# A reordered attention-and-experts kernel: new places in its fixed order, routing by pairs of batches, a product in 64-row tiles, late weights asked for earlier

## The chip, the cores and the metric

The kernel runs on one core of one Trainium2 chip. The metric is the device time of one execution in microseconds (us), the median of the runs shown. TensorE is called PE, VectorE DVE, ScalarE ACT, GpSimd POOL and SyncE SP, as in the profile.

## The reference

A Nyström attention over 8 batches of 8 heads, 576 positions and 64 features is followed by a layer of 8 experts. `q_lm` and `k_lm` are means over 18 neighbouring positions (32 landmarks).

```python
A = sm(q, k_lm); Bm = sm(q_lm, k_lm); C = sm(q_lm, k)      # softmax of scaled scores
Z = Bm.T / (norm1(Bm) * norminf(Bm) + 1e-6)
for _ in range(6):
    Z = 2 * Z - Z @ Bm @ Z                                  # Newton steps
x = (A @ Z @ C @ v)                                         # heads side by side: 4608 x 512
logits = x @ w_gate                                         # 8 experts
e = argmax(logits); gate_w = softmax(logits)[e]; eom = sigmoid(x @ w_output_gate)[e]
out = gate_w * eom * (relu(x @ w1[e]) @ w2[e])              # each token through its one expert
```

All tensors are float32. `w1` is 8 x 512 x 1024 and `w2` is 8 x 1024 x 512.

## The kernel before

The kernel has two stages. The first computes attention and routing. It works in 16 **units** (`u`): a batch and one half of its heads (4 heads on 4 x 32 partitions). `load_qk` and `load_v` bring the unit's q, k and v through the SP queue. `sums` adds groups of positions to landmarks on POOL (k) and DVE (q). `turn3` transposes three 128 x 128 pieces at a time on PE and `keep3` copies them from PSUM on ACT (nine transposes and three copies each for q and k). `c_scores`, `c_max`, `c_exp`, `c_turn`, `c_keep`, `values` and `keep_values` make C v; `a_scores` to `a_back` make the normalized A, transposed back, which stays in `ATs` until its batch is done.

Per **batch** (`b`), `b_scores` to `b_c` make B. `p_mm` and `p_next` are seven Newton steps, each a set of 32 x 32 matmuls on PE and an update on DVE. `z_blocks` spreads the result into block-diagonal form (`ZB`) on POOL; `z_turn`, `gates` and `logits` compute the gate logits straight from it. `x_mm` computes rows of x, 128 at a time in five pieces (the last of 64 rows), `x_out` converts them to bf16 on ACT and writes them to the DRAM table `x_rows`. `choose` finds the expert of each token, `count` adds counts on POOL, `ranks` and `places` find each token's place among its expert's tokens, `onehot` makes the matrices St, and `coef_in` to `coef` make the two factors of a token and write them to `x_rows` too.

After attention comes a closing part: from the counts, the first tile of each expert (`base`), each token's tile (`pj`), and with St a product `pinv` that inverts the placing, so that `gat_i` holds for each of 43 tiles of 128 places the row of `x_rows` to fetch. `tile_w` holds each tile's expert.

The second stage goes over 36 to 43 tiles. `load` gathers 128 rows by an indirect DMA on POOL's queue, `turn_x`, `up`, `turn` and `down` run the two matrix products in bf16, and an indirect DMA scatters the rows to `out`.

All weights stand in one SBUF tensor, `wall`, of eight slots of 2 MB. Slots 4 to 7 serve as **homes** of attention's buffers first: q and k (`nats`), partial sums (`t9s`), v (`vSs`) and the matrices of `ATs`. `load_expert(e)` asks for an expert's weights on POOL's queue, casting to bf16; each request stands behind what still reads its slot.

What sets the order: every step is a small function, recorded with a place. The list is sorted by place and each engine's instructions stand in that order; an engine's queue is strictly in order, and nothing is moved afterwards. A unit is `P = 12` places long; for example

```python
at(t - P + 1.5 + 0.4 * n, turn3, u, 0, n)
at(t + 0.0, c_scores, u)
at((NU + 4) * P if e == E - 4 else u * P + P + 3.3, lambda e=e, u=u: load_expert(e, ATs[u]))
```

The closing part is not in the list; it is recorded behind all of it. `load_expert` begins with two one-element casts from a tile that a late step writes, which hold the requests back: experts 0 to 3 at units 1, 3, 5 and 7, experts 5 to 7 after unit 15, expert 4 after the last product.

PSUM has eight banks: two for scores (`s`), two for transposes (`t`), two for small products (`m`, two buffers), one for Newton (`n`) and one for x (`px`).

Of the kernel before, what the change touches and what calls it, by code (L numbers as in the profile page):

```python
# [22 lines left out]
F32 = mybir.dt.float32  # L23
# [14 lines left out]
def kernel(  # L38
# [37 lines left out]
    def load_expert(e, after):  # L76

        for c in (0, W1):
            nc.gpsimd.tensor_copy(wall[:1, e, c:c + 1], after[:1, :1])
        nc.gpsimd.dma_start(out=wall[:, e, :W1].rearrange("p (c f) -> p c f", f=F),  # L80
                            in_=moe_w1[e].rearrange("(c p) f -> p c f", p=128))
        nc.gpsimd.dma_start(out=wall[:, e, W1:].rearrange("p (c d) -> p c d", d=HD),
                            in_=moe_w2[e].rearrange("(c p) d -> p c d", p=128))
# [20 lines left out]
    nc.gpsimd.iota(pcol, pattern=[[1, 1]], base=0, channel_multiplier=1, allow_small_or_imprecise_dtypes=True)  # L104
    tok = gp.tile([128, B, TB], F32)
# [5 lines left out]
    cum = gp.tile([128, T + 1, E], BF16)  # L111
    nc.vector.memset(cum[:, 0], 0.0)
    oh = gp.tile([128, T, E], BF16)
# [12 lines left out]
    lgs = [gp.tile([128, TB, m], F32, name=f"lg{i}") for i in range(2)]  # L126
# [17 lines left out]
    with tc.tile_pool(name="attn_c", bufs=1) as cp, \  # L144
# [4 lines left out]
        mask64 = cp.tile([128, HH, D], F32)  # L149
        nc.vector.memset(mask64, 0.0)  # L150
        for h in range(HH):
            nc.vector.memset(mask[h * m:(h + 1) * m, h, :], 1.0)
            nc.vector.memset(mask64[h * m:(h + 1) * m, h, :], 1.0)
        bones = mask.rearrange("p h l -> p (h l)")
        wgs = cp.tile([128, HH, 2 * E], F32)
        for hf in range(2):
            nc.sync.dma_start(out=wgs[hf * D:(hf + 1) * D, :, :E],
                              in_=moe_w_gate[hf * HH * D:(hf + 1) * HH * D].rearrange("(h d) e -> d h e", d=D))
            nc.sync.dma_start(out=wgs[hf * D:(hf + 1) * D, :, E:],
                              in_=moe_w_output_gate[hf * HH * D:(hf + 1) * HH * D].rearrange("(h d) e -> d h e", d=D))  # L160
# [9 lines left out]
        nats = [home(E - 1 - i // 3 * 2, i % 3, GD).rearrange("p (k d) -> p k d", d=D) for i in range(6)]  # L170
        t9s = [home(e, 6, GD // 2).rearrange("p (k d) -> p k d", d=D) for e in (E - 1, E - 3)]
        VD = HH * VJ * D
        vSs = [home(E - 2, i, VD)[:VA * m].rearrange("p (h j d) -> p h j d", h=HH, j=VJ) for i in range(2)]
# [86 lines left out]
        def values(u):  # L260
            nc.vector.reciprocal(sts[u][:, 2:3], sts[u][:, 1:2])
            sts[u, 0] = pV = ps.tile([128, 192], F32, tag="m", bufs=2, name="pV")
# [47 lines left out]
        def b_scores(b):  # L310
            pBs[b] = pB = ps.tile([128, 2, m], F32, tag="m", bufs=2, name="pB")
# [21 lines left out]
        def b_cols(b):  # L333
            pBs[b] = pS = ps.tile([128, 2, m], F32, tag="m", bufs=2, name="pS")
            nc.tensor.matmul(pS, lhsT=bones, rhs=XWs[b][:, :, :W])
# [28 lines left out]
        def z_blocks(b):  # L364
            ZBs[b] = sb.tile([128, 2, HH, D], F32, tag="ZB", name="ZB")
            for hf in range(2):
                nc.gpsimd.tensor_tensor(
                    ZBs[b][:, hf], mask64,
                    XWs[b][:, hf, :].rearrange("p (h d) -> p h d", h=1).to_broadcast([128, HH, D]), op=MUL)


        def z_turn(b):
            ZTs[b, 0] = pZ = ps.tile([128, 192], F32, tag="m", bufs=2, name="pZ")
# [6 lines left out]
        def gates(b, hf):  # L380
            ZTs[b, hf] = pG = ps.tile([128, 2 * E], F32, tag="m", bufs=2, name="pG")
            for h in range(HH):
                nc.tensor.matmul(pG[hm(h), :], lhsT=ZTs[b][hf * D:(hf + 1) * D, hm(h)],
                                 rhs=wgs[hf * D:(hf + 1) * D, h, :])

        def keep_gates(b, hf):
            nc.scalar.copy(Gs[b % 2][:, hf, :2 * E], ZTs.pop((b, hf)))

        def logits(b):
            pLs[b] = pL = ps.tile([128, TB, m], F32, tag="m", bufs=2, name="pL")  # L390
# [8 lines left out]
        def choose(b):  # L399
            lg, t0, t1, pL = lgs[b % 2], b * TB, (b + 1) * TB, pLs.pop(b)  # L400
# [3 lines left out]
            sm = sms[b] = sb.tile([128, 8, TB], F32, tag="sm", name="sm")  # L404
            w3 = w3s[b] = sb.tile([128, 2, TB, E], F32, tag="w3", name="w3")
            ohb = oh[:, t0:t1]
            nc.vector.tensor_reduce(sm[:, 0], lg[:, :, :E], axis=X, op=MAX)
            nc.vector.tensor_tensor(w3[:, 0], lg[:, :, :E], b_e(sm[:, 0], TB), op=ALU.is_ge)
            nc.vector.scalar_tensor_tensor(out=w3[:, 0], in0=w3[:, 0], scalar=-8.0, in1=b_t(e8, TB),
                                           op0=MUL, op1=ADD)  # L410
            nc.vector.tensor_reduce(sm[:, 1], w3[:, 0], axis=X, op=ALU.min)
            nc.vector.tensor_tensor(ohb, b_t(row[:, :E], TB), b_e(sm[:, 1], TB), op=ALU.is_equal)
            nc.vector.memset(ohb[64:, TB - 1], 0.0)
# [6 lines left out]
        def ranks(b):  # L420
            t0, t1 = b * TB, (b + 1) * TB
            prk = prks[b] = ps.tile([128, TB, E], F32, tag="m", bufs=2, name="prk")
            prf = prk.rearrange("p t e -> p (t e)")
            nc.tensor.matmul(prf, lhsT=U, rhs=oh[:, t0:t1].rearrange("p t e -> p (t e)"), start=True, stop=False)
            nc.tensor.matmul(prf, lhsT=ones, rhs=cum[:, t0:t1].rearrange("p t e -> p (t e)"),
                             start=False, stop=True)

        def places(b):
            t0, t1, sm, w3 = b * TB, (b + 1) * TB, sms[b], w3s.pop(b)
            nc.vector.tensor_tensor(w3[:, 1], prks.pop(b), oh[:, t0:t1], op=MUL)  # L430
            nc.vector.tensor_reduce(sm[:, 2], w3[:, 1], axis=X, op=ADD)
            smi = sb.tile([128, 2, TB], I32, tag="smi")
# [3 lines left out]
            nc.vector.tensor_copy(pjl[:, t0:t1], smi[:, 1])  # L436
            nc.vector.scalar_tensor_tensor(out=psl[:, t0:t1], in0=pjl[:, t0:t1], scalar=-128.0, in1=sm[:, 2],
                                           op0=MUL, op1=ADD)
            nc.vector.memset(psl[64:, t1 - 1:t1], -1.0)

        def onehot(b):
# [7 lines left out]
        def coef_in(b):  # L449
            lg = lgs[b % 2]  # L450
            wc = wcs[b] = sb.tile([128, 2, TB, E], F32, tag="wc", name="wc")
            nc.gpsimd.tensor_tensor(wc[:, 0], lg[:, :, :E], b_e(sms[b][:, 0], TB), op=SUB)
            nc.gpsimd.tensor_tensor(wc[:, 1], lg[:, :, E:2 * E], oh[:, b * TB:(b + 1) * TB], op=MUL)

        def coef_exp(b):
            nc.scalar.activation(out=wcs[b][:, 0], in_=wcs[b][:, 0], func=EXP)

        def coef_sum(b):
            nc.vector.tensor_reduce(sms[b][:, 3:5].rearrange("p a t -> p (a t)"),
                                    wcs.pop(b).rearrange("p a t e -> p (a t) e"), axis=X, op=ADD)  # L460

        def coef_exp2(b):
            nc.scalar.activation(out=sms[b][:, 5], in_=sms[b][:, 4], func=EXP, scale=-1.0)

        def coef(b):
            sm, t0, t1 = sms.pop(b), b * TB, (b + 1) * TB
            nc.vector.scalar_tensor_tensor(out=sm[:, 6], in0=sm[:, 5], scalar=1.0, in1=sm[:, 3], op0=ADD, op1=MUL)
            pay = sb.tile([128, TB, 2], F32, tag="pay")
            nc.vector.reciprocal(pay[:, :, 0], sm[:, 6])
            nc.gpsimd.tensor_copy(pay[:, :, 1], tok[:, b])  # L470
            nc.sync.dma_start(
                out=x_rows[t0 * 128:t1 * 128, HD // 2:].rearrange("(t p) c -> p t c", p=128), in_=pay)
# [5 lines left out]
        def x_mm(b, j):  # L478
            pX = pXs[b, j] = ps.tile([128, HD], F32, tag="px", name="pX")
            for hf in range(2):  # L480
                nc.tensor.matmul(pX[:tk(j), hf * HH * D:(hf + 1) * HH * D],  # L481
                                 lhsT=ATs[2 * b + hf][:, j * 128:j * 128 + tk(j)],
                                 rhs=ZBs[b][:, hf].rearrange("p h d -> p (h d)"))

        def x_out(b, j):
            xo = sb.tile([128, HD], BF16, tag="xo", bufs=3)
            nc.scalar.copy(xo[:tk(j)], pXs.pop((b, j))[:tk(j)])  # L487
            r0 = (b * TB + j) * 128
            nc.sync.dma_start(out=x_rows[r0:r0 + tk(j), :HD // 2], in_=xo[:tk(j)].bitcast(F32))


        plan = []

        def at(place, fn, *args):
            plan.append((place, len(plan), fn, args))

        P = 12.0
        for u in range(NU):
            t = u * P
            at(t - 4 * P + 11.9 if u > 2 else -30 + u, load_qk, u)  # L500
            at(t - 2 * P + 11.9 if u > 1 else -30 + u + 0.5, load_v, u)
            for n in range(3):
                at(t - P + 1.5 + 0.4 * n, turn3, u, 0, n)
                at(t - P + 2.6 + 0.5 * n, keep3, u, 0, n)
# [244 lines left out]
```

## Time and profile before

| | |
|---|---|
| median of 3 runs | 456.54 us (454.12 to 457.53) |
| profiled execution: its time | 459.6 us |
| profiled execution: its span | 457.8 us |
| granted PE clock, mean | 0.917 |
| busy PE, DVE, ACT, POOL | 359.2, 250.3, 160.0, 221.8 us |
| read from and written to HBM | 67.58 MB, 15.25 MB |

Busy time is the time in which at least one instruction of the engine ran, so overlapping matmuls are counted once. The slices cut the span in 40 parts of 11.4 us with the busy tenths of each. In a group's line, the count after x is of instructions (a float32 matmul appears as two), then the busy us and the mean ns of one, and behind the bar the engine's idle time just before them with what ended it. "Issue" means that nothing the profile shows was waited for.

### The profile page before, as it was taken

How to read it: one execution, taken by the hardware profiler on the slowest of the kernel's cores; microseconds unless marked ns; L12 is line 12 of the kernel's file. 1: busy time of each engine (PE TensorE's matmuls, PEld its weight loads, DVE VectorE, ACT ScalarE, POOL GpSimd, SP SyncE). 2: the span in 40 equal slices, each digit the busy share in tenths (PEclk: the TensorE clock that was granted, in tenths of full speed). 3: DMA queues.
4: the chain of work that ended last, by engine and by line, in shares of the span. 5: the costliest groups of instructions: out<-in, count | busy, mean ns of one | idle time of the engine just before them, and what ended most of it. 6: DMA issues, size and time to landing. Idle time of an engine off the chain costs nothing.

```text
span 457.8 us, 11307 instructions
## 1 busy us (share of the span) xinstructions
PE 359.2 (78%) x4264; PEld 212.0 (46%) x4283; DVE 250.3 (55%) x657; ACT 160.0 (35%) x373; POOL 221.8 (48%) x327
## 2 busy tenths in 40 slices
PE   0767687887888888888784534899999999999790
PEld 0444455555555555555452322455555555555450
DVE  1267766986869788686653331344544344444340
ACT  1445454455545645564321200222222222222110
POOL 2555758285672736563542255145454455444321
PEclk9878989999989999999888555999999999999996
DMA  6965999969799665321199994022222322233211
GB/s 145 251 227 168 226 262 207 263 166 233 217 243 255 175 180 139 114 48 59 27 189 222 212 215 138 24 83 93 103 95 80 105 94 92 93 95 104 74 52 37
DMA packets 41353, 66.44 MB, mean 145 GB/s; under 512 B 9953, under 2 KB 29410, under 8 KB 41282
## 3 DMA queue, kind: packets, MB, share of 16 engines
q0 software_dynamic: 17648, 31.90, 31.5%
q1 hardware_dynamic: 23634, 33.64, 26.1%
q8 instruction: 39, 0.64, 0.6%
q14 instruction: 32, 0.26, 0.2%
HBM read 67.58 MB, written 15.25 MB: 181 GB/s over the span
## 4 chain that ended last, share of the span: by engine, by line
PE 42%; DVE 21%; issue 11%; DMA 10%; POOL 7%; ACT 5%; SPq 1%; POOLq 0%; ACTq 0%; DVEq 0%
PE ph L656 13%; PE py L675 12%; DMA out_dram<-ysb 6%; PE pX L481 3%; PE pht L666 3%; DMA wall<-in_q_dram 3%; PE p L234 2%; DVE ax L287 2%; DVE At L284 2%; POOL At L290 2%; PE pV L266 2%; ACT ECT L258 2%; PE pt L642 2%; DVE st L243 2%; PE pN L349 2%
## 5 line engine op out<-in xcount | busy, mean ns | idle before, releaser
L660 ACT ACTIVATE h<-ph 128x512 bf16<-128x512 f32 x76 | 41.3, 594 | 139.4 <-PE ph L656 139.4
L682 POOL DMA_INDIRECT out_dram<-ysb x38 | 38.5, 1013 | 85.5 <-DVE ysb L681 85.5
L656 PE MATMUL ph<-wall,xT 128*128 x303 | 74.9, 391 | 4.9 <-issue 2.6
L210 PE MATMUL pT<-I,wall 128*128 128x128 f32 x288 | 50.1, 307 | 32.1 <-ACT tr L214 15.4
L675 PE MATMUL py<-wall,hT 128*128 x286 | 67.9, 379 | 0.9
L214 ACT COPY tr<-pT 128x384 f32<-128x384 f32 x96 | 43.3, 480 | 44.4 <-PE pT L210 44.3
L210 PEld LDWEIGHTS pT<-I,wall 128*128 128x128 f32 x288 | 33.9, 153 | 46.4 <-ACT tr L214 25.9
L481 PE MATMUL pX<-ZB,wall 128*128 128x256 f32 (+1 forms) x160 | 48.4, 430 | 6.3 <-ACT xo L487 6.3
L656 PEld LDWEIGHTS <-xT 128*128 128x128 bf16 x304 | 30.3, 100 | 42.7 <-issue 8.7
L634 POOL DMA_INDIRECT xs<-x_rows,gat_i x43 | 41.8, 972 | 16.0 <-issue 11.0
L668 DVE COPY hT<-pht 128x1024 bf16<-128x1024 bf16 x38 | 26.3, 691 | 39.1 <-PE pht L666 38.5
L290 POOL TENSOR_TENSOR At<-At,ax 128x576 f32<-128x576 f32 x16 | 18.6, 1161 | 55.8 <-DVE ax L287 55.8
L675 PEld LDWEIGHTS <-hT 128*128 128x128 bf16 x304 | 28.2, 98 | 27.1
L680 DVE CAST ysb<-xs 128x1 int32<-128x1 f32 x38 | 5.7, 153 | 55.6 <-DMA out_dram<-ysb 23.2
L481 PEld LDWEIGHTS pX<-ZB,wall 128*128 128x128 f32 (+1 forms) x160 | 28.0, 196 | 15.1 <-ACT xo L487 8.6
L487 ACT CAST xo<-pX 128x512 bf16<-128x512 f32 (+1 forms) x40 | 23.3, 583 | 27.9 <-PE pX L481 21.2
L681 DVE TENSOR_SCALAR ysb<-py,xs 128x512 f32<-128x512 f32 x38 | 28.3, 745 | 8.1 <-PE py L675 7.5
L197 POOL TENSOR_TENSOR wall<-wall 128x576 f32<-128x576 f32 x16 | 22.4, 1402 | 12.2 <-DMA wall<-in_k_dram 12.2
L300 POOL TENSOR_TENSOR At<-At,ax 128x576 f32<-128x576 f32 x16 | 18.5, 1156 | 19.7 <-DVE ZV L361 8.0
L349 PE MATMUL pN<-nxt 32*32 32x96 f32 x768 | 26.9, 257 | 0.5 <-DVE nxt L358 0.5
L234 PE MATMUL p<-tr,lmT 64*32 64x288 f32 x512 | 25.7, 462 | 0.8 <-ACT lmT L224 0.5
L349 PEld LDWEIGHTS pN<-nxt 32*32 32x32 f32 x768 | 16.1, 108 | 20.7 <-issue 9.0
(143 smaller groups left out, 546.1 us busy)
## 6 DMA issues: line engine op xcount, KB each, us to landing
wall<-in_moe_w_dram POOLq DMA_DIRECT2D x16, 1024.0 KB, 19.2
wall<-in_k_dram SPq DMA_DIRECT2D x16, 576.0 KB, 6.7
wall<-in_q_dram SPq DMA_DIRECT2D x16, 576.0 KB, 8.2
wall<-in_v_dram SPq DMA_DIRECT2D x48, 192.0 KB, 4.7
x_rows<-xo SPq DMA_DIRECT2D x32, 128.0 KB, 5.9
xs<-x_rows,gat_i POOLq DMA_INDIRECT x43, 4.1
out_dram<-ysb POOLq DMA_INDIRECT x38, 2.8
x_rows<-St SPq DMA_DIRECT2D x1, 516.0 KB, 4.9
```

Of the source, the lines that this page charges most:

```text
L210: nc.tensor.transpose(pT[:, k2], identity=I128, in_=nat[:, 6 * n + 2 * k2:6 * n + 2 * k2 + 2].rearrange("p k d -> p (k d)"))
L214: nc.scalar.copy(tr[u, i][:, 3 * n:3 * n + 3], tr.pop((u, i, n)))
L234: nc.tensor.matmul(p[hm(h), i, :NC], lhsT=lms[i * D:(i + 1) * D, hm(h)], rhs=rhs)
L290: nc.gpsimd.tensor_tensor(Ats[u], Ats[u], b_l(axs[u][:, 0]), op=SUB)
L349: nc.tensor.matmul(pN[hm(h), hf, :], lhsT=cur[hm(h), hf, :W], rhs=cur[hm(h), hf, :])
L481: nc.tensor.matmul(pX[:tk(j), hf * HH * D:(hf + 1) * HH * D], lhsT=ATs[2 * b + hf][:, j * 128:j * 128 + tk(j)], rhs=ZBs[b][:, hf].rearrang ...
L634: nc.gpsimd.indirect_dma_start(out=xs, out_offset=None, in_=x_rows, in_offset=bass.IndirectOffsetOnAxis(ap=gat_i[:, j:j + 1], axis=0))
L656: nc.tensor.matmul(ph[hf], lhsT=xT[:, dc, :], rhs=wf[:, bass.ds(we[j] + (dc * F + hf * 512), 512)], start=(dc == 0), stop=(dc == DCH - 1))
L660: nc.scalar.activation(out=hs[j][:, hf * 512:(hf + 1) * 512], in_=ph[hf], func=RELU)
L675: nc.tensor.matmul(py, lhsT=hT[:, fc, :], rhs=wf[:, bass.ds(we[j] + (W1 + fc * HD), HD)], start=(fc == 0), stop=(fc == FCH - 1))
L681: nc.vector.tensor_scalar(out=ysb[:, :HD], in0=py, scalar1=xs[:, HD // 2:HD // 2 + 1], scalar2=None, op0=MUL)
L682: ins = nc.gpsimd.indirect_dma_start(out=out, out_offset=bass.IndirectOffsetOnAxis(ap=token, axis=0), in_=ysb[:, :HD], in_offset=None, bou ...
```

## The change

- **Places.** All steps take their places from one table `PLACE`, with entries of their own for the last (`!`) and the one before the last (`?`) unit, batch or group. The closing part is cut into steps (`counts`, `full_tiles`, `starts`, `tiles`, `slot_cols`, `slot_tiles`, `slots`, `slot_rows`, `tile_experts`) that are in the list as well.
- **Routing.** `choose`, `ranks`, `places` and the coefficients run over groups of two batches; the last two batches are groups of one. Counts are no longer added on POOL: `oh` has a sixth, empty column per batch, `ranks` adds shifted copies in PSUM by twelve (six) matmuls, and `places` adds the running count on DVE.
- **x.** `ZB` holds two heads per 64 rows instead of four per 128. A piece of x is four matmuls over 64 rows and 128 columns, in pairs on the upper and lower half of the array into two PSUM banks; two pieces go together into one copy pair and one write. `px` has two banks, `m` one buffer. `gates` uses one set of matmuls in place of two.
- **Late weights.** The casts in `load_expert` are gone. Homes move: q and k to slots 6 and 4, v to 5, transposed q and k (`tr`) to three homes in 7; `ATs` get a pool of seven buffers. Experts 4, 6, 7 and 5 are asked for at places 181.7, 182.2, 186.0 and 192.5 (unit 15 begins at 180).
- **Start.** k and q of unit 0 are first in the SP queue, ahead of the gate weights.

```diff
-    def load_expert(e, after):
-        for c in (0, W1):
-            nc.gpsimd.tensor_copy(wall[:1, e, c:c + 1], after[:1, :1])
+    def load_expert(e):
...
-        nats = [home(E - 1 - i // 3 * 2, i % 3, GD).rearrange("p (k d) -> p k d", d=D) for i in range(6)]
+        nats = [home(E - 2 - i // 3 * 2, i % 3, GD).rearrange("p (k d) -> p k d", d=D) for i in range(6)]
-        vSs = [home(E - 2, i, VD)[:VA * m].rearrange("p (h j d) -> p h j d", h=HH, j=VJ) for i in range(2)]
+        vSs = [home(E - 3, i, VD)[:VA * m].rearrange("p (h j d) -> p h j d", h=HH, j=VJ) for i in range(2)]
-                tr[u, i] = sb.tile([128, K2, 128], F32, tag="tr", bufs=4, name="tr")
+                tr[u, i] = home(E - 1, (2 * u + i) % 3, GD).rearrange("p (k c) -> p k c", k=K2)
-            ATs[u] = home(E - 4, u % 7, S)
+            ATs[u] = sb.tile([128, S], F32, tag="AT", bufs=7, name="AT")
-            pBs[b] = pB = ps.tile([128, 2, m], F32, tag="m", bufs=2, name="pB")
+            pBs[b] = pB = ps.tile([128, 2, m], F32, tag="m", name="pB")
...
-            ZBs[b] = sb.tile([128, 2, HH, D], F32, tag="ZB", name="ZB")
+            ZBs[b] = sb.tile([128, 2, 2, D], F32, tag="ZB", name="ZB")
...
+        groups = [(b, b + 1) for b in range(0, B - 2, 2)] + [(B - 2,), (B - 1,)]
...
-        def count(b):
-            for t in range(b * TB, (b + 1) * TB):
-                nc.gpsimd.tensor_tensor(cum[:, t + 1], cum[:, t], oh[:, t], op=ADD)
...
+        def ranks(r):
+            nb = len(groups[r])
+            ns = nb * (TB + 1)
...
+            for l in range(ns):
+                nc.tensor.matmul(to[:, l * E:], lhsT=ones if l else U, rhs=at_[:, :(ns - l) * E],
+                                 start=(l == 0), stop=(l == ns - 1))
+        def places(r):
...
+            nc.vector.tensor_tensor(bt(w3[:, 1]), prk[:, :, :TB], bt(b_t(cum[:, r], nt)), op=ADD)
+            nc.vector.tensor_tensor(cum[:, r + 1], cum[:, r], prk[:, nb - 1, TB], op=ADD)
...
-        def x_mm(b, j):
-            pX = pXs[b, j] = ps.tile([128, HD], F32, tag="px", name="pX")
-            for hf in range(2):
-                nc.tensor.matmul(pX[:tk(j), hf * HH * D:(hf + 1) * HH * D],
-                                 lhsT=ATs[2 * b + hf][:, j * 128:j * 128 + tk(j)],
-                                 rhs=ZBs[b][:, hf].rearrange("p h d -> p (h d)"))
+        def x_mm(b, j0):
+            pX = pXs[b, j0] = ps.tile([128, 2, 2, 2, 2 * D], F32, tag="px", name="pX")
+            for j in range(j0, min(j0 + 2, TB)):
+                for hf in range(2):
+                    for i in range(2):
+                        pr = slice(i * D, (i + 1) * D)
+                        nc.tensor.matmul(pX[:tk(j), i, j - j0, hf], lhsT=ATs[2 * b + hf][pr, j * 128:j * 128 + tk(j)],
+                                         rhs=ZBs[b][pr, hf].rearrange("p h d -> p (h d)"))
...
+            xo = sb.tile([128, 2, HD], BF16, tag="xo")
...
+        PLACE = {
+            "load_qk": -36.3, "load_v": -14.6, "turn3 0 0": -11.2, "turn3 0 1": -10.3, "turn3 0 2": -10.0,
+            "keep3 0 0": -10.7, "keep3 0 1": -9.2, "keep3 0 2": -7.1, "turn3 1 0": -7.1, "turn3 1 1": -6.5,
...
+            "load_expert 0": 29.3, "load_expert 1": 52.9,
+            "load_expert 2": 78.3, "load_expert 3": 113.9, "load_expert 4": 181.7, "load_expert 5": 192.5,
+            "load_expert 6": 182.2, "load_expert 7": 186.0, "x_mm 0!": 38.9, "a_sum!": 8.3, "a_sum?": 7.4,
...
+        }
```

More of the change, by code (lines that the diff above doesn't have):

```diff
@@ L125 @@
         in_=blank.bitcast(F32).rearrange("p (b c) -> p b c", b=1).to_broadcast([64, B, XR // 2]))
[L126 removed]
+    lgs = [gp.tile([128, 2, TB, m], F32, name=f"lg{i}") for i in range(2)]
     for lg in lgs:
@@ L403, in choose, with lg_ @@
             nc.vector.transpose(out=lg[:64, TB - 1], in_=pL[:64, TB - 1])
[L404 to L409, printed above, removed]
+        def lg_(r, e0):
+            return lgs[r % 2][:, :len(groups[r])].rearrange("p b t e -> p (b t) e")[:, :, e0:e0 + E]
@@ new lines, in counts, with full_tiles @@
+        def counts():
+            pBs[B] = pn = ps.tile([E, 128], F32, tag="m", name="pn")
+            nc.tensor.matmul(pn, lhsT=cum[:, len(groups)], rhs=first)
+        def full_tiles():
+            ni = sb.tile([E, 128], I32, tag="ni", bufs=1)
+            nc.vector.tensor_scalar(out=ni, in0=pBs[B], scalar1=127.0, scalar2=None, op0=ADD)
+            nc.vector.tensor_scalar(out=ni, in0=ni, scalar1=7, scalar2=None, op0=ALU.logical_shift_right)
+            Bs[B] = sb.tile([E, 128], F32, tag="nf", bufs=1, name="nf")
+            nc.vector.tensor_copy(Bs[B], ni)
@@ new lines, in slot_tiles, with slots @@
+        def slot_tiles(a):
+            nc.gpsimd.tensor_tensor(tr[a][:, :, 1], lm[a],
+                                    row[:, a + 1:a + TQ + 1].rearrange("p (t j) -> p t j", j=1).to_broadcast([128, TQ, J]),
+                                    op=MUL)
+        def slots(a):
+            if a == 0:
+                pAs[B] = ps.tile([128, 2, J], F32, tag="px", name="pinv")
+            for t in range(TQ):
+                nc.tensor.matmul(pAs[B].rearrange("p a j -> p (a j)"), lhsT=St[:, a + t],
+                                 rhs=tr[a][:, t].rearrange("p a j -> p (a j)"),
+                                 start=(a + t == 0), stop=(a + t == T - 1))
@@ new lines @@
+        for b in range(B):
+            for fn in (b_scores, b_max, b_exp, b_norm, b_cols, b_c, z_blocks, z_turn, z_keep, gates, keep_gates, logits):
+                at("batch", b, B, fn)
+            for it in range(7):
+                at("batch", b, B, p_mm, it)
+                at("batch", b, B, p_next, it)
+            for j in range(0, TB, 2):
+                at("batch", b, B, x_mm, j)
+                at("batch", b, B, x_out, j)
+            at("batch", b, B, keep_logits)
+        for r, bs in enumerate(groups):
+            for fn in (choose, ranks, places, coef_in, coef_exp, coef_sum, coef_exp2, coef):
+                at("group", r, len(groups), fn)
+            for i in range(len(bs)):
+                at("group", r, len(groups), onehot, i)
@@ L563 @@
+        for e in range(E):
+            at("end", 0, 0, load_expert, e)
+        last = (NU - 1) * P
+        for fn in (counts, full_tiles, starts, tiles, slot_rows, tile_experts):
+            plan.append((last + PLACE[fn.__name__], len(plan), fn, ()))
+        for i in range(4):
+            for fn in (slot_cols, slot_tiles, slots):
+                plan.append((last + PLACE[f"{fn.__name__} {i}"], len(plan), fn, (i * TQ,)))
         with tc.manual_schedule():
```

331 lines of the change are left out of this document (157 added, 174 removed), and 14 rows, old and new, of the table PLACE.

## The prediction

> **What bounds the kernel now.** I read the page's slices first, then busy time by stage, then the timeline of the joint between the stages, then groups by shape and waits. The slices show three parts: attention (slices 1 to 20), a hole (slices 21 to 24), the experts (25 to 39).
>
> ```profile
> PE   0767687887888888888784534899999999999790
> PEclk9878989999989999999888555999999999999996
> DMA  6965999969799665321199994022222322233211
> ```
>
> Busy time in seven stretches follows: start, stretch from us, length, then PE, PEld, DVE, ACT, POOL, granted clock, DMA share, GB/s.
>
> ```profile
> 12.70:81.60 68.90, 52.27 (x829) 32.64 (x833) 43.62 (x102) 33.20 (x81) 44.85 (x63) 0.88 0.89 223
> 81.60:215.80 134.20, 111.56 (x2003) 71.68 (x1996) 106.41 (x291) 72.60 (x185) 73.92 (x123) 0.99 0.70 175
> 227.70:240.00 12.30, 10.38 (x158) 6.61 (x146) 5.73 (x25) 2.90 (x9) 6.43 (x18) 0.84 1.04 171
> 240.00:268.70 28.70, 15.07 (x102) 9.29 (x102) 12.44 (x43) 4.55 (x12) 8.77 (x18) 0.65 1.22 218
> 268.70:280.40 11.70, 0.59 (x4) 0.46 (x5) 0.81 (x5) 0.00 (x0) 8.24 (x9) 0.50 0.94 200
> 280.40:457.80 177.40, 160.75 (x1041) 86.28 (x1059) 69.95 (x147) 41.25 (x76) 72.07 (x73) 0.95 0.25 82
> ```
>
> 81.6 and 215.8 are the first reductions over the scores (L243) of units 5 and 15, so the second row is 10 units: 13.42 us each, 26.84 per batch. PE is busy 83% of it and DVE 79%: neither is full, the order and its waits share the bound. In units 0 to 4 (first row) the DMA engines are at 0.89. The rows from 240.0 to 280.4 are the hole: 40.4 us between the last Newton matmul and the first expert matmul. The timeline says why (start us, us, engine, line, idle before):
>
> ```profile
> 260.48 0.81 POOL L80 DMA_DIRECT2D wall<-in_moe_w_dram  x1 [13.21 <-issue]
> 262.20 1.77 POOL L596 TENSOR_TENSOR Va<-oj,row 128x430 bf16<-128x430 bf16 x2
> 268.49 0.20 DVE L608 SCALAR_TENSOR_TENSOR gat_i<-sl 128x43 int32<-128x43 f32 x1
> 269.72 1.07 POOL L634 DMA_INDIRECT xs<-x_rows,gat_i  x1 [3.10 <-issue]
> 278.63 0.59 PE L642 MATMUL pt<-Ib,xs 128*128 128x128 bf16 x4 [10.91 <-issue]
> ```
>
> POOL stands 13.2 us at the weight request of expert 4, whose home holds the matrices that the last product reads until 259.9. The routing table's multiply (L596) is behind it in POOL's queue. The first gather, issued at 269.72, lands only at 278.6, behind the 2 MB asked for at 260.5.
>
> **The change part by part.** The sum is made against the profiled execution: span 457.8, its time 459.6 us. The median of the runs shown is 456.54, 3.1 us lower.
>
> *Start.* The SP queue now issues k and q of unit 0 ahead of the small transfers.
>
> ```profile
> 0.81 0.76 SPq L157 DMA_DIRECT2D wgs<-in_moe_w_gate_dram  x1
> 4.82 2.08 SPq L184 DMA_DIRECT2D wall<-in_k_dram  x1
> ```
>
> That is up to 4.0 us earlier. Units 1 to 3 wait for bytes, so some comes back; I take -3 (bounds -4, -1). The first units keep their 68.9 us: they are DMA-bound and hold no product.
>
> *Product x in two 64-row tiles.* The groups by shape:
>
> ```profile
> L481 PE MATMUL pX<-ZB,wall 128*128 128x256 f32 x128 | 38.1, 425 | 5.3 <-ACT xo L487 5.3
> L234 PE MATMUL p<-tr,lmT 64*32 64x288 f32 x512 | 25.7, 462 | 0.8 <-ACT lmT L224 0.5 <-ACT EC L247 0.3
> ```
>
> L481 takes 38.1/32 = 1.19 us for one row tile: two matmuls of 256 columns, 430 columns per us. L234, on 64*32 tiles, streams 8 x 288 columns in 25.7/32 = 0.80 us: 2870 per us, 6.7 times as many with 8 tiles, so tiles do run side by side. The new form streams 4 x 128 columns on two tiles: 0.60 us if they overlap wholly, 0.71 at L234's 84%, 1.19 if not at all. I take 0.65, nearest L234. Five per batch save 2.7 us of PE. TensorEngine Tiling (Array Packing) of the Trainium skill, Tiling Modes, says that changing the tiling mode drains the array; that speaks against three visits per batch to a new mode. The trace shows idle of 0.25 to 0.33 us before weight loads at such joints, so by it up to 6 x 0.3 = 1.8 us per batch would go back, PE would be the fuller engine again at 21.7 us, and the time would be some 434. I don't add it, since the old form had joints with L349 and L234 of its own. POOL loses half of L367 (about 0.5 us per batch); ACT copies the same elements in as many pieces.
>
> *Routing by two batches.* DVE's choose (five operations near 0.20 us), places (seven near 0.17) and coefficients (0.24, 0.16, 0.19) run once per two batches on twice the elements; rows of 40 elements take 0.20 us and of 64 take 0.22, so a doubled one costs some 0.23. Places gains two additions of 0.2. Per batch: choose 1.0 to 0.6, places 1.1 to 0.8, coefficients 0.6 to 0.3: -1.0 us of DVE. POOL loses five counts of 0.2 per batch. PE gets twelve rank matmuls per two batches where it had four; at 0.10 (a weight load, L425) to 0.19 (L424) this adds 0.2 to 0.8 us per batch, I take 0.4. Merged gate matmuls save 0.1.
>
> *The period.* Per batch PE goes from 111.56/5 = 22.3 to 19.9 us, DVE from 21.3 to 20.3. DVE becomes the fuller engine. At the old share of the busiest engine (22.3/26.84 = 83%) the period is 20.3/0.83 = 24.4. All places move as well; one wait that they visibly address is this one:
>
> ```profile
> PE pT L210 <- ACT tr L214: 9.5, 16, 1.1
> ```
>
> In the window 94.8 to 202.5 PE waits 9.5 us for its own transposes' copies, 2.4 per batch, because all nine come in a row with two buffers; the new order parts them by other work. I credit 0.9 of it: 23.5 us. Bounds: 26.8 (places give nothing, DVE waits as before) and 21.4 (DVE 95% full). Five batches: 5 x 3.3 = -16.7. The same bytes must come: 155, 223 and 175 GB/s over the three stretches to 215.8 make 40.8 MB; 250 GB/s at a full share (175/0.70) needs 163 us, so 196 is reachable, but batches with a weight load already took 28.0 where others took 26.4 us. Four of those: I give back 3. Net -13.7 (bounds 0, -24).
>
> *Last unit and Newton iterations.* 215.8 to 240 keeps its seven steps; the products of batch 6 beside them shrink by half (four of 1.1 us to 0.6) and seven steps of 0.53 (PE) and 0.35 (DVE) are 6.2 us of 12.3: -2.5 (bounds 0, -5).
>
> *The tail.* From the last Newton matmul to the gather's rows, by durations of before: last update 0.35, turn 0.38, copy 0.33, gates 0.33, copy 0.28, logits 0.9, two transposes 0.5, choose 1.25, ranks 0.8, places 1.9, sum and tile counts 1.0, start matmul and one-hot 1.3, base, spread, reduce and add 1.4, four slot columns at L592's and L595's means 4 x 1.41 = 5.7, the last L596 1.0, ten matmuls 0.9, four closing operations 1.05: 19.4 us against 28.7. The products and copies of batch 7 lie between these on PE and ACT. Nothing on POOL's queue waits for the product now: expert 4's request is placed after the last reads of unit 14's q and k. -9.3 (bounds -5, -12).
>
> *Late weights and the first gather.* Experts 4 and 6 are asked for ahead of unit 15's subtraction on POOL (220.96 before), so 42 us ahead of the gather; with 215 GB/s of the slices after 229 us that is 9.0 MB, and 8.4 MB of weights plus 1.2 MB of product rows are wanted. They are nearly through. The gather took 268.7 to 278.6; free it costs 1.1 of issue and the page's median 4.1. I take 7 of 9.9: -2.9 (bounds 0, -4.7). The Trainium skill, DMA: Bandwidth & Descriptors, Queues, rings and completion order, says that an engine consumes the descriptors of one ring in order; the 8.9 us from issue to landing here agrees, and by it the gather cannot overtake the weights (with all 9.6 MB ahead of it, 44.7 us at 215 GB/s, it would land 2.7 us later than free).
>
> *Homes.* Transposed q and k get three homes in the wall for four buffers. The next writer of a home stands some five places after its reader, so I put it at nothing; without that cover PE would wait a score set, 0.8 us, in each of 16 units. A moves to buffers of its own, seven as before; the one-cell casts ahead of each weight request (0.3 us on POOL) go.
>
> *Experts.* Lines unchanged; 177.4 us stays.
>
> **Sum:** -3 - 13.7 - 2.5 - 9.3 - 2.9 = -31.4; 459.6 - 31.4 = 428.2, less 3.1 for the median: **425 us**.
>
> **The rivals.**
> *A, only the joints gain.* Tiles or places give the stretch of ten units nothing: the first rows' waits for DMA and for POOL (L290) stay. For: 26.4 us also in batches with no weight load and DMA at 0.5. Against: PE's own 2.4 us less. -3 - 0 - 1 - 9.3 - 1 = -14: 442.
> *B, the order pays more.* The period falls to 21.4 and the tail to 17: -3 - 24 - 4 - 12 - 4 = -47: 409. The DMA floor of 163 us stands just under it.
> *C, slower: the one-buffer PSUM tile.* Tag m falls from two buffers to one to pay for the product's second bank. Values, scores of B, columns, turn, gates, logits and ranks pass through it: 7.5 uses per batch, 60 in all. If PE, in order, waits at each for a copy queued late on ACT or DVE, everything behind it in PE's queue, transposes above all, waits too, and ACT and DVE for those. My 31 us are gone from 0.52 us per use; at 0.8 us it is 48 - 31 = 17 slower: 473. For: PE already waits up to 1.2 us for copies on ACT (pV for ECT, 4 times in that window). Against: in the new order each writer's reader stands before the next writer, mostly a whole step before.
> *D, the change does nothing.* If homes were freed as late as before, POOL would stand again and the order cancel out: 456. The order of POOL's queue, with no request behind the last product, speaks against it.
>
> **How the numbers follow.** My forecast 0.62, A 0.15, B 0.11, C 0.08, D 0.04. The forecast's own range, 413 to 438; to leave out no more than two in ten it reaches to A and B: 406 to 447. About 1% can be told from no change here. Forecast, A and B are faster by more: 0.88. D is same: 0.04. C is slower: 0.08.
>
> **What would show it.** Right: first transpose near 9 us; L243 every 11.8 us in mid attention; product busy about 26 us in place of 48; no POOL wait over 5 us at a weight request; 19 us from the last Newton matmul to the gather table; experts still 177 us. Wrong: a unit period above 13, idle of PE put down to readers of tag m, product busy near 48, or gathers that land over 9 us after issue.

## The result, and the profile after

The changed kernel takes 439.67 us (median of 4 runs, 438.62 to 442.59), beside 455.76 us for the kernel before on the same chip: a ratio of 0.966, 95% interval 0.960 to 0.972. It is faster, as forecast, by 16 us instead of 31; the time lies in the stated range of 406 to 447, but outside the forecast's own range of 413 to 438, and near the figure of rival A (442), though not by rival A's way. The profiled execution took 440.14 us with a span of 438.4, where the one before had 459.6 and 457.8; the stages below therefore differ by 19.4 us in sum, not by 16.

The slices of the changed kernel (11.0 us each), PE, granted clock and DMA share:

```profile
PE   5578698978888997977385346999999999999790
PEclk9968999989999699978655558999999999999996
DMA  6965999979979964219999331222322223323311
```

PE still has a hole, though a shorter one: the granted clock is down at 0.5 to 0.6 for five slices around it (208 to 263 us), and the DMA engines are full for four (197 to 241 us). Busy time by stretch, with the columns of the table before (start and end, length, PE, PEld, DVE, ACT, POOL, clock, DMA share, GB/s):

```profile
72.87:197.40 124.53, 106.55 (x2065) 71.96 (x2063) 100.89 (x263) 69.68 (x180) 72.94 (x96) 0.94 0.79 194
197.40:206.10 8.70, 6.79 (x146) 4.62 (x142) 6.96 (x19) 4.44 (x12) 4.71 (x8) 0.89 1.13 181
206.10:226.50 20.40, 12.54 (x183) 9.02 (x182) 7.50 (x29) 2.88 (x9) 4.07 (x7) 0.58 1.23 217
226.50:249.90 23.40, 12.13 (x119) 9.07 (x115) 13.61 (x42) 4.10 (x12) 5.12 (x9) 0.50 0.91 167
249.90:257.90 8.00, 0.62 (x5) 0.48 (x6) 1.89 (x8) 0.00 (x0) 4.62 (x5) 0.50 0.24 61
257.90:438.40 180.50, 160.99 (x1041) 86.12 (x1059) 69.31 (x148) 41.25 (x76) 75.67 (x77) 0.95 0.26 83
```

The boundaries are the same events as before: the first score reductions of units 5 and 15, the first and last Newton step of batch 7, the gather table, the first expert matmul. Set against the forecast, in us:

| stage | before | forecast | after |
|---|---|---|---|
| start to unit 15 | 215.8 | 199.1 | 197.4 |
| unit 15 to the last Newton step | 24.2 | 21.7 | 29.1 |
| last Newton step to gather table | 28.7 | 19.4 | 23.4 |
| table to first expert matmul | 11.7 | 8.8 | 8.0 |
| experts | 177.4 | 177.4 | 180.5 |

The units gave what was forecast and a little more. Against the forecast 12.0 us are missing: 7.4 in the second row, which should have shrunk and grew, 4.0 in the third and 3.1 in the last, less what the others gained. The first part of the second row in the kernel before, up to the first Newton step of batch 7 (the stretch that is missing among the seven of the prediction), was

```profile
215.80:227.70 11.90, 8.57 (x153) 5.04 (x149) 9.02 (x29) 4.25 (x11) 4.62 (x7) 0.88 0.13 35
```

and is now 8.7 us. So the whole loss of that row lies in the Newton steps, 20.4 us where they took 12.3. The timeline there (start us, us, engine, line, operation; in brackets the idle time before and who ended it):

```profile
218.01 1.07 ACT L512 CAST xo<-pX 128x512 bf16<-128x512 f32 x2 [10.53 <-DMA x_rows<-xo]
219.13 2.08 PE L504 MATMUL pX<-ZB,AT 64*128 64x128 f32 x16 [6.60 <-ACT xo L512]
236.07 1.07 ACT L512 CAST xo<-pX 128x512 bf16<-128x512 f32 x2 [7.19 <-DMA x_rows<-xo]
```

ACT stands 10.5 us for a free row buffer, which a write to `x_rows` still holds. PE stands 6.6 us behind it, at a product whose PSUM tile ACT has not emptied, and the Newton steps of batch 7 stand behind that product in PE's queue. Eighteen us later it happens again. The waits of ACT in the whole span (us in total, times, longest):

```profile
ACT xo L512 <- DMA x_rows<-xo: 21.8, 4, 10.5
```

In the kernel before the same wait came to 6.4 us. The four weight requests now stand at 194.95, 196.64, 202.81 and 207.19 us, and from then on the DMA engines are full while batches 6 and 7 write their rows.

### The profile page after: what moved, and what is told of

It reads as the page before. It is cut to its first block, busy times and chain, and to the rows that moved or that the text cites. A ratio compares the mean times of both kernels' runs of the same rounds, so it can differ in the third digit from the quotient of the medians.

```text
span 438.4 us, 11408 instructions
## 1 busy us (share of the span) xinstructions
PE 351.8 (80%) x4393; PEld 214.9 (49%) x4412; DVE 245.5 (56%) x623; ACT 156.1 (36%) x367; POOL 210.4 (48%) x262
## 4 chain that ended last, share of the span: by engine, by line
PE 42%; DVE 23%; DMA 15%; issue 6%; POOL 6%; ACT 3%; SPq 1%; another core or an unknown queue 1%; POOLq 0%; ACTq 0%
PE ph L718 13%; PE py L737 11%; DMA x_rows<-xo 7%; DMA out_dram<-ysb 6%; PE pht L728 3%; PE pX L504 3%; POOL At L291 3%; PE pN L350 2%; DVE wall L198 2%; PE p L235 2%; DMA wall<-in_q_dram 2%; DVE wall L199 2%; PE pV L267 2%; DVE st L244 2%; DVE ax L288 2%
## 5 line engine op out<-in xcount | busy, mean ns | idle before, releaser
L215 ACT COPY wall<-pT 128x384 f32<-128x384 f32 x96 | 44.3, 486 | 51.1 <-PE pT L211 50.5
L211 PE MATMUL pT<-I,wall 128*128 128x128 f32 x288 | 51.8, 313 | 13.2 <-DMA wall<-in_k_dram 9.7
L504 PE MATMUL pX<-ZB,AT 64*128 64x128 f32 (+1 forms) x320 | 31.1, 344 | 11.5 <-ACT xo L512 11.5
L291 POOL TENSOR_TENSOR At<-At,ax 128x576 f32<-128x576 f32 x16 | 19.5, 1220 | 35.6 <-DVE ax L288 35.6
L350 PE MATMUL pN<-nxt 32*32 32x96 f32 x768 | 28.4, 268 | 6.0 <-DVE nxt L359 5.8
L301 POOL TENSOR_TENSOR At<-At,ax 128x576 f32<-128x576 f32 x16 | 18.5, 1155 | 29.5 <-DVE st L262 17.8
L504 PEld LDWEIGHTS pX<-ZB,AT 64*128 64x128 f32 (+1 forms) x320 | 25.1, 228 | 15.3 <-ACT xo L512 12.6
L512 ACT CAST xo<-pX 128x512 bf16<-128x512 f32 (+1 forms) x48 | 22.2, 515 | 26.6 <-DMA x_rows<-xo 21.8
L728 PEld LDWEIGHTS <-h 128*128 128x128 bf16 x304 | 20.6, 99 | 12.6 <-ACT h L722 3.0
L235 PE MATMUL p<-wall,lmT 64*32 64x288 f32 x512 | 26.2, 470 | 0.6 <-ACT lmT L225 0.5
```

Of the source, the lines that this page charges most:

```text
L211: nc.tensor.transpose(pT[:, k2], identity=I128, in_=nat[:, 6 * n + 2 * k2:6 * n + 2 * k2 + 2].rearrange("p k d -> p (k d)"))
L215: nc.scalar.copy(tr[u, i][:, 3 * n:3 * n + 3], tr.pop((u, i, n)))
L235: nc.tensor.matmul(p[hm(h), i, :NC], lhsT=lms[i * D:(i + 1) * D, hm(h)], rhs=rhs)
L291: nc.gpsimd.tensor_tensor(Ats[u], Ats[u], b_l(axs[u][:, 0]), op=SUB)
L350: nc.tensor.matmul(pN[hm(h), hf, :], lhsT=cur[hm(h), hf, :W], rhs=cur[hm(h), hf, :])
L504: nc.tensor.matmul(pX[:tk(j), i, j - j0, hf], lhsT=ATs[2 * b + hf][pr, j * 128:j * 128 + tk(j)], rhs=ZBs[b][pr, hf].rearrange("p h d -> p ...
```

## The experiments

My theory T was then: the late weights, asked for earlier, share the DMA engines with the writes of x, these land late, and two row buffers are too few to hide it. R1 blamed the low clock; R2 said that 8.4 MB of weights are a floor whatever else is done.

**1. Five row buffers**

```diff
-            xo = sb.tile([128, 2, HD], BF16, tag="xo")
+            xo = sb.tile([128, 2, HD], BF16, tag="xo", bufs=5)
-            ATs[u] = sb.tile([128, S], F32, tag="AT", bufs=7, name="AT")
+            ATs[u] = sb.tile([128, S], F32, tag="AT", bufs=5, name="AT")
-            Vt = tr[a] = sb.tile([128, TQ, 2, J], BF16, tag="Vt", bufs=4, name="Vt")
+            Vt = tr[a] = sb.tile([128, TQ, 2, J], BF16, tag="Vt", bufs=3, name="Vt")
```

> The changed kernel with five buffers for the converted rows of x in place of two (room comes from the A buffers, 7 to 5, and from one buffer of the closing part). Theory T: the late weights share the DMA engines with the writes of x, each write takes some 10 us to land, ACT stands 21.1 us for a free buffer, and PE's products and Newton steps stand behind it. T expects these waits under 3 us in sum, the seven Newton steps of batch 7 in 13 us or less where they took 20.4, and about 429 us where the changed kernel has 439.7. Rival R1: PE's lower granted clock (0.55 to 0.86 there) stretches that part, and the waits of ACT lie beside it: the steps stay above 18 us and the time above 437. Rival R2: the 8.4 MB of late weights are a floor of their own: the first expert matmul cannot come before about 243 us of the span whatever the buffers, so at most 15 us are to be had, and less if the weights come later.

431.27 us, a ratio of 0.948 to the kernel before (0.940 to 0.956), which lies below the changed kernel's interval. No wait of ACT is put down to a write any more (4.0 us in two waits have no named cause). The stretches of this run, from the first Newton step of batch 7 to the first expert matmul, in the columns above:

```profile
206.00:218.60 12.60, 9.73 (x183) 6.71 (x182) 7.41 (x29) 2.97 (x9) 4.26 (x7) 0.81 1.25 221
218.60:237.60 19.00, 10.85 (x115) 7.89 (x115) 13.47 (x42) 4.11 (x12) 5.14 (x9) 0.59 1.23 223
237.60:248.30 10.70, 0.60 (x5) 0.46 (x6) 1.94 (x9) 0.00 (x0) 4.77 (x5) 0.50 0.90 168
```

The Newton steps take 12.6 us for 20.4, and the tail 19.0 us for 23.4; the forecast had said 19.4. The clock in the Newton stretch rises from 0.58 to 0.81 with no change aimed at it: here it went with PE's waits. R1 falls. Of the 12.2 us won here, 2.7 go back in the third row: the table is ready at 237.6, and the gather lands only at 246.1. That is R2's share, though the weights' queue is not the only wait in it. The gather reads the rows, and the chain that ended last shows the last write of rows (start us, us):

```profile
229.06 11.94 DMA x_rows<-xo
```

It lands at 241.0, after the table, and POOL issues the gather at 242.3, 4.7 us after the table. Without late weights (experiment 2) it issues 2.2 us after it.

**2. No late weights**

```diff
-        for e in range(E):
+        for e in range(E - 4):
             at("end", 0, 0, load_expert, e)
-            nc.vector.tensor_scalar(out=tile_w[:, :J], in0=ej, scalar1=float(E - 1), scalar2=float(WE),
+            nc.vector.tensor_scalar(out=tile_w[:, :J], in0=ej, scalar1=float(E - 5), scalar2=float(WE),
```

> The changed kernel without the four late weight requests; tiles of experts 4 to 7 go through the weights of expert 3, so that the same matmuls run. T: writes of x land in 3 to 4 us, ACT's waits for them go, Newton steps of batch 7 take 12 us or less, the tail about 19 us, the first expert matmul stands at about 243 us of the span where it stood at 257.9: about 425 us. R1: the clock is as low as before, nothing moves by more than 3 us: 437 to 443. R2 expects what T expects here or a little more.

422.69 us in a single run. The Newton steps take 12.7 us, the tail 18.1, and the first gather lands 5.3 us after its table; the first expert matmul stands at 245.1. The time from issue to landing of the rows' writes, by the view of that line, is in this run

```profile
DMA to landing us min/median/max: 2.3/3.6/11.0
```

and in the changed kernel

```profile
DMA to landing us min/median/max: 2.5/6.7/17.3
```

Both are over all 24 writes. Of the eight issued from 190 us on, beside the late weights, the median is 7.9 us in the changed kernel and 2.8 here, and the first of them, issued at 200.6 us, takes 17.3 us there and 3.9 here. So the writes land nearly three times as late beside the weights, and that is all that two buffers needed. In experiment 1 they land as late as in the changed kernel (median 8.7 from 190 us on); ACT no longer waits for them, only the gather does. T holds in both directions. Of the 17.0 us between this run and the changed kernel, 8.4 are the buffers' (experiment 1). Of the rest, 2.6 lie between table and first matmul, 0.9 in the tail, and 5.6 in the experts' stage (175.9 us against 181.5), where five experts share one slot's weights here; that part I can't put down to the late weights.

**3. The product in whole-array matmuls again**

```diff
-                    for i in range(2):
-                        pr = slice(i * D, (i + 1) * D)
-                        nc.tensor.matmul(pX[:tk(j), i, j - j0, hf], lhsT=ATs[2 * b + hf][pr, j * 128:j * 128 + tk(j)],
-                                         rhs=ZBs[b][pr, hf].rearrange("p h d -> p (h d)"))
+                    nc.tensor.matmul(pX[:tk(j), j - j0, hf].rearrange("p i c -> p (i c)"),
+                                     lhsT=ATs[2 * b + hf][:, j * 128:j * 128 + tk(j)],
+                                     rhs=ZBs[b][:, hf].rearrange("p h d -> p (h d)"))
```

(with `ZB` and its mask of four heads, as before the change, and A in six buffers)

> The changed kernel with the product x in whole-array matmuls again (128 rows by 256 columns, ZB of 256 columns, mask of four heads); two pieces still share the PSUM banks, the copies and the write; A has six buffers in place of seven. The prediction's step: the product costs PE 2.7 us more per batch and POOL 0.5 us; with PE the fuller engine again the period grows by 1.0 to 2.7 us per batch, the time by 8 to 20 us: 448 to 460. Rival: DVE and the order set the period, and the freed PE time was idle time; the time stays within 3 us of the changed kernel's.

451.97 us, ratio 0.993 (0.989 to 0.997): the tiles are worth 12.3 of the 16 us. The product's line in this run, and then in the changed kernel, from the groups (count, busy us, mean ns, idle before):

```profile
L502 PE MATMUL pX<-ZB,AT 128*128 128x256 f32 (+1 forms) x160 | 47.7, 446 | 13.8 <-ACT xo L511 13.8
```

```profile
L504 PE MATMUL pX<-ZB,AT 64*128 64x128 f32 (+1 forms) x320 | 31.1, 344 | 11.5 <-ACT xo L512 11.5
```

The units from 5 to 15 take 131.5 us here and 124.5 with the tiles. The rival, that freed PE time is idle time, falls: 7.0 us of units for some 10 us of PE. The rest of the 12.3 us is not PE time of the units: the Newton steps of batch 7 took 22.9 us in this run (20.4 with the tiles) and the tail 24.3 (23.4), again with waits of ACT for writes (18.2 us in all).

**4. Routing for one batch at a time**

```diff
-        groups = [(b, b + 1) for b in range(0, B - 2, 2)] + [(B - 2,), (B - 1,)]
+        groups = [(b,) for b in range(B)]
-    cum = gp.tile([128, B, E], F32)
+    cum = gp.tile([128, B + 1, E], F32)
```

> The changed kernel with routing for one batch at a time (eight groups of one, at the places that a group has). The prediction's step: DVE gets back 1.0 us per batch and is the fuller engine, so the period grows by 0.5 to 1.0 us: 443 to 447 us. Rival: these DVE operations fall into its idle time; within 2 us of the changed kernel's.

440.80 us, ratio 0.971 (0.962 to 0.980): not to be told from the changed kernel. The trace tells more than the time. DVE is busy 108.6 us between units 5 and 15 where it was 100.9, and unit 15 comes at 202.3 us where it came at 197.4, which would make pairing worth 4.9 us up to there. How far one trace can be trusted in this is shown by experiments 1, 7 and 8, whose kernels are the same up to the late weights: their unit 11 stands at 147.5, 150.0 and 150.7 us. So the work on DVE is sure, and the 4.9 us are not known to better than some 3. The difference doesn't show in the time, since the Newton steps of batch 7 took 12.4 us in this run, against 20.4: ACT's waits for writes came to 17.6 us here, where they were 21.8, and lay elsewhere. The expectation's step points the right way in the units, and its total was missed.

**5. The new places alone**

```diff
-            at(t + 0.0, c_scores, u)
...
+            for fn in (turn_lm, keep_lm, c_scores, c_max, c_exp, a_scores, a_max, a_sub, a_exp, a_sum, a_mul, a_back,
+                       values, keep_values):
+                by(u, NU, t, fn)
```

(`by` looks a step up in the new table; the rest of the kernel before stays)

> The kernel before with the new places for the steps of units and of Newton's method alone (loads, transposes, scores, softmaxes, values, B, Newton, spreading and turning its result; the last unit's way back of A keeps its old place); gates, product, routing, homes, weights and the closing part stay as before. The prediction credited the places with 0.9 us per batch: 134.2 us from unit 5 to unit 15 become some 129, and about 448 us in all. Rival A: the places give that stretch nothing (133 or more), as the run with the whole-array product hints, which has all of the change but the tiles and takes 131.5 us there: 454 to 457. Where the places do help is then ahead of unit 5, where the changed kernel is 5.5 us faster from unit 3 to unit 5.

455.52 us, ratio 0.996 (0.993 to 1.000): no difference that can be told. Units 5 to 15 take 132.8 us for 134.2, unit 15 comes 2.6 us earlier. The credit of 0.9 us per batch was too much; it is 0.3, and that lies within what two traces of one kernel differ by. For the places, in the kernel before, rival A was right. The ten units in this run, and then in experiment 6, which has the old places (columns as above):

```profile
80.47:213.23 132.76, 113.92 (x1984) 76.62 (x1982) 102.00 (x292) 72.61 (x185) 76.34 (x125) 0.95 0.71 178
79.14:212.40 133.26, 109.89 (x1989) 71.05 (x1986) 106.43 (x292) 72.71 (x185) 74.95 (x126) 1.00 0.71 178
```

With the new places alone the granted clock fell to 0.95, where it was 0.99 in the kernel before and 1.00 in experiment 6, and PE is busy 2 to 4 us longer with the same matmuls. Every run with the new places had 0.92 to 0.96 there. Against the kernel before, PE's idle time fell by 3.8 us (22.6 to 18.8) and its busy time rose by 2.4. So most of what the places won in waits was lost in slower matmuls, which the lower clock fits; why it is lower isn't shown.

**6. The start alone**

```diff
         wgs = cp.tile([128, HH, 2 * E], F32)
+        nc.vector.memset(wgs, 0.0)
```

> The kernel before with one more instruction: the gate weights' tile is cleared first, as in the changed kernel, so that its four transfers wait and k of unit 0 goes first in the SP queue (q of unit 0 behind them). The prediction's step: unit 0 starts 4 us or more earlier and 3 us of it stay: units 1 to 3 are 2.5 to 3 us earlier and the time is about 452.5. Rival: bytes bound the first units and the later batches, so the 3 us are waited for again: 455 to 456.

453.54 us, ratio 0.994 (0.991 to 0.997): 2.8 us by the ratio (1.5 to 4.0), 1.7 by the medians (455.28 before), near the 3 of the step. Unit 1 comes 1.7 us earlier and unit 15 3.4.

**7. Experts 4 and 6 asked for earlier still, with five buffers**

```diff
-            "load_expert 4": 181.7, ... "load_expert 6": 182.2,
+            "load_expert 4": 171.0, ... "load_expert 6": 174.6,
```

> The changed kernel with five row buffers, and experts 4 and 6 asked for 10.7 and 7.6 places earlier, right after the last reads of their homes (171.0 and 174.6). T with the floor: the weights begin some 9 us earlier, in a stretch where the DMA engines are at a third, and are through by about 234 us of the span; the first gather lands 5.3 us after its table as in the run without late weights, where it took 8.5: 427 to 429 us. Rival: reads of q, k and v and the writes of x of batches 5 and 6 are slowed instead, or POOL stands at the requests: 431 or more.

429.75 us, ratio 0.941 (0.934 to 0.947). The requests came 6 and 5 us earlier, at 189.0 and 191.5, not 9. The gather landed 5.4 us after its table, as without late weights. But unit 15 came at 200.1 us in this run, against 196.5 in experiment 1, and took back what the gather won. The earlier requests can't have made most of that: unit 11 stood 2.5 us later already (150.0 for 147.5), 39 us ahead of the first request. The intervals of the two overlap; both beat the changed kernel, and which is better stays open.

**8. All late weights 24 places later, with five buffers**

```diff
-            "load_expert 4": 181.7, "load_expert 5": 192.5, "load_expert 6": 182.2, "load_expert 7": 186.0,
+            "load_expert 4": 205.7, "load_expert 5": 216.5, "load_expert 6": 206.2, "load_expert 7": 210.0,
```

> The changed kernel with five row buffers, and all four late weight requests 24 places later (205.7 to 216.5). T with the floor: 8.4 MB need 39 us at 215 GB/s, and the gather of the first tile stands behind them in the same queue; asked for some 20 us later they are through at about 260 us of the span, and the first expert matmul comes at about 264: about 446 us, though attention ends earlier than in any run with early requests. Rival R1 (weights are hidden anyway, the clock decides): 431 as with the early requests.

446.31 us in a single run. The table is ready at 243.2, and the first expert matmul comes at 267.1. In the chain, the first gather takes 17.9 us from its issue at 247.2:

```profile
247.19 17.87 DMA xs<-x_rows,gat_i
```

POOL's queue shows what the later gathers wait for:

```profile
255.01 0.94 POOL L696 DMA_INDIRECT xs<-x_rows,gat_i  x1 [1.69 <-DMA wall<-in_moe_w_dram]
260.01 0.95 POOL L696 DMA_INDIRECT xs<-x_rows,gat_i  x1 [4.06 <-DMA wall<-in_moe_w_dram]
264.93 0.94 POOL L696 DMA_INDIRECT xs<-x_rows,gat_i  x1 [3.97 <-DMA wall<-in_moe_w_dram]
```

So asking early is right in itself: it is worth 15 us against this run, once the rows have room to wait in.

## Why the prediction was right or wrong

**Start (-3): right.** The SP queue's first lines after:

```profile
0.81 0.41 SPq L185 DMA_DIRECT2D wall<-in_k_dram  x1
1.28 0.42 SPq L185 DMA_DIRECT2D wall<-in_q_dram  x1
```

The first transpose stands at 4.9 us instead of 12.7, nearly twice the 4.0 us that were counted; of these 7.8 us 2.4 are left in unit 1 and 3.2 in unit 3, as bytes are waited for. Experiment 6 measured 2.8 in the time (1.7 by the medians).

**Units (-13.7, before unit 15): right in sum, by other terms, and partly by luck.** Unit 15 came 18.4 us earlier, where start and units together were to give 16.7. But the ten units themselves gave 9.7 us of the 13.7, and 8.7 came ahead of unit 5, where 3 were forecast. Against the changed kernel's or the old unit 15, the runs show 7.4 us for the tiles (204.8 less 197.4), 4.9 for pairing, 3.4 for the start and 2.6 for the places. That they add up to 18.3 is no proof of the single terms, since equal kernels differ by up to 3 us there. The tiles' saving was taken somewhat too large. Two pieces in tiles, and then two in the whole array (experiment 3), where the clock was full:

```profile
121.09 1.16 PE L504 MATMUL pX<-ZB,AT 64*128 64x128 f32 x16
142.18 1.93 PE L502 MATMUL pX<-ZB,AT 128*128 128x256 f32 x8
```

That is 0.58 us a piece for 0.97. The 1.19 of the prediction was a mean over all pieces, at low clock too; by the same mean a piece in tiles took 24.9/32 = 0.78 us (0.65 taken). Over the ten units the product's busy time on PE fell from 27.1 to 16.4 us, 2.1 per batch for the 2.7 taken. The twelve rank matmuls take 0.5 us per pair of batches (0.8 more per pair was taken). DVE per batch came to 20.2 us, as forecast (20.3). PE came to 21.3, not 19.9. Its granted clock in this stretch was 0.94 where it had been 0.99; if busy time goes by the clock, 106.6 us would be 101.2 at the old one, 20.2 per batch. That I did not foresee; experiment 5 shows that it came with the places. The period became 24.9 us and not 23.5 (24.1 with the 3 us that were given back), since the places gave 0.3 instead of 0.9 and PE remained the fuller engine. The waits show that the one wait which the new order addresses did go (11.6 us for its own copies between units 5 and 15, none now), and where it went:

```profile
PE pM L220 <- ACT ECT L259: 5.9, 6, 1.6
PE pN L350 <- DVE nxt L359: 4.8, 7, 1.4
PE pE L254 <- ACT wall L215: 3.8, 8, 0.9
```

Had the 5.5 us between units 3 and 5 not come, which I had put at nothing since they were "DMA-bound", the sum would have been short. I didn't separate their cause.

**Mode changes.** The prediction weighed the rule of the Trainium skill (TensorEngine Tiling (Array Packing), Tiling Modes) that changing the tiling mode drains the array. With the idle times that it took for this, 9 us would have been lost. In the trace the idle time just before the product's weight loads is 1.2 us in all over the ten units (0.7, 0.3 and 0.2 in the waits of that stretch), where 0.3 us at each of 15 visits would be 4.5. The joints behind the visits I didn't separate, but the tiles' 12.3 us speak against a loss of that size.

**Last unit and Newton steps (-2.5): the step that failed.** It became +4.9, a miss of 7.4 us. I counted the products beside these steps and forgot the cover of their writes: the 1.2 MB of rows appeared only as bytes ahead of the gather. What a write costs when it is hidden, and how many of them the two buffers hide (each twice as large as one of the three before), was never asked. Rival C asked the right kind of question of the wrong buffer: not PSUM tag m, but the row buffers behind ACT. Experiments 1 and 2 show it.

**Tail (-9.3): the sum of durations was right, its cover not.** It took 23.4 us instead of 19.4; with five buffers it took 19.0, without late weights 18.1. Two more waits for writes lay in it (7.2 and 3.3 us on ACT). The first held back a product on PE until 239.3 us, and the matmul for the first tile of each expert (`starts`) stands behind that product in PE's queue. The second lay beside DVE's work on the slot columns and is not on the chain.

**Late weights and gather (-2.9): right in size, for another reason than the one given.** Table to matmul took 8.0 us (8.8 forecast). The gather was not held up here because the table itself was late; in experiment 1, with the table 12 us earlier, it landed 8.5 us after it, 3.2 more than without late weights. Of these, 2.5 lie ahead of its issue, where it waited for the last write of rows, which the prediction did not have as a wait.

**Experts (0): +3.1.** From the third set of transposes of this stage to the fourth it took 7.3 us, and 7.6 to 8.7 in experiments 1 to 4; it took 3.8 in the kernel before. ACT and DVE stand there together:

```profile
ACT h L722 <- remote: 5.4, 1, 5.4
DVE hT L730 <- remote: 5.4, 1, 5.4
```

"Remote" means that the trace knows no event in the kernel that ended the wait. DVE's is there without late weights too (5.2 us in experiment 2), so it isn't they. In the six runs that have it (the changed kernel, experiments 1 to 4 and 7) the first expert matmul comes 5.8 to 6.0 us after the first gather's issue, and DVE goes on 15.5 to 15.7 us after that issue. Where the first matmul comes 8 to 20 us after it (the kernel before, experiments 5, 6 and 8), the wait is not there; in experiment 8 the stage takes 177.5 us, as before. So an earlier first matmul may be partly lost again here. What takes these 15.6 us stays open.

## What to carry to other kernels

When a transfer is moved earlier, list every other transfer that will then run beside it, and for each how many buffers its producer has until it must stand: bytes that fit in the total can still stop an in-order engine. Here writes that land in some 8 us rather than 3 cost 8 us more with two buffers than with five, and with five it was the last one, which nothing covers, that still held up its reader. A sum of durations for a serial tail (19.4 us) met 19.0 and 18.1 once no write held it up, so a tail that is much longer than its sum is a sign of a wait to be looked for. A stage's start in a single trace moved by up to 3 us between equal kernels, so smaller differences of single traces prove little.

## What the runs showed that I had not expected

- Two float32 matmuls on the two 64-row halves really run side by side: at full clock a piece of x costs 0.58 us instead of 0.97 in experiment 3, a factor of 1.7, with weight loads and all.
- The granted clock of PE stood at 0.94 in the units of the changed kernel and 0.99 in those of the kernel before, with PE busy a larger share (86% and 83%), and the new places alone brought it to 0.95. In a stretch of waits it fell to 0.58, and rose to 0.81 when only the waits were taken away.
- A reordering of nearly every step of attention, alone, made no difference that could be told (0.996, 0.993 to 1.000).
